# Chunk 1's keys crossed by GpSimd, a subtraction that restores the key order, and a new order of the first layers' calls, in a sorted-block attention with a two-layer MLP

## The chip, the cores and the metric

The kernel runs on one core of a Trainium2 chip. The metric is the device time of one execution in microseconds (us), lower is better. The engines are called PE (matmul), DVE (VectorE), ACT (ScalarE), POOL (GpSimd) and SP (SyncE, which here only issues DMAs).

## The reference

There are 4 batches, 8 heads, 768 positions and a head size of 64. Positions are cut into 8 blocks of 96. A small 8x8 matrix per head is balanced five times and mixes the blocks of keys and of values; each block of queries then attends to its mixed block. The result, as 3072 tokens of 512 numbers, goes through two matrix products with `h * cos(h)` between them.

```
P = sort_net
for _ in range(5):
    P = P - max(P, -1); P = exp(P)
    P = P / (sum(P, -1) + 1e-9); P = P / (sum(P, -2) + 1e-9)
k_sorted = einsum('bhij,bhjcd->bhicd', P, k_b)      # v_sorted likewise
scores = q_b @ k_sorted_b.T / sqrt(64)
attn = softmax(scores); x = attn @ v_sorted_b       # (3072, 512)
h = x @ w_in                                        # 512 -> 2048
out = (h * cos(h)) @ w_out                          # 2048 -> 512
```

## The kernel before

The tokens are worked in eight chunks of 384: chunk n is half of batch n // 2, four blocks of 96 tokens, called u. The order of all instructions is written out by hand; the engines run their own queues in that order and wait for each other by semaphores. PSUM is split into three "big" buffers of two banks (`B`) and two "acc" buffers of one bank (`C`), each handed out in turn.

For each chunk and block: `qk` (or two `qk_half`) makes scores on PE, DVE takes the maximum over the keys (`mx`, line 486) and subtracts it (`s`, line 487), `expo` writes exp of it to a `p_buf` on ACT (line 511), the result is turned (`p_transpose` on PE with a copy to `pT` by DVE or ACT in chunks 0 and 1, a DMA transpose issued by SP later), `av` multiplies it with the mixed values and DVE normalizes it (`r`, line 555, and `xn`, line 557), and `x_transpose` turns it into `xT`. Then `up(n, fp, lo, hi)` is an eighth of the first layer: PE makes `h` in a big buffer, ACT writes `c` = cos(h) (line 592), DVE multiplies `gg` = c * h (line 595). `down(n, ts, half)` is half of a 128-token tile of the second layer in an acc buffer, and ACT or DVE copies it out. In each chunk the attention of the next one is put between these calls. Chunk 0's first layer runs in two halves of columns (two blocks each), so that it can start before all its blocks are attended to.

Mixed keys: `k_products` makes for each pair of key positions t a [128, ...] block in PSUM whose partitions hold two neighbouring positions x of 64 head dimensions, for even and odd heads e. The tile `kTs` keeps them in three slots. A product for an even head reads slots 0 and 1, for an odd head slots 1 and 2, so slot 1 holds the other position of either kind, in the opposite partition half. For batch 0, `k_sort_0` copies from PSUM in four pieces of 64 partitions: chunk 0's with ih = 0, chunk 1's with ih = 1. `z_keys` zeroes on POOL the halves that these pieces leave out. For the later batches, `k_sort_1` and `k_sort_g` copy whole PSUM blocks into slots 0 and 2 and `k_swap` fills slot 1 by two DMAs.

Chunks 0 and 1 have the keys of a block in the order (x t), position parity first, in scores and in `s`; `expo` puts them back in the order (t x) as it writes.

Queries: `load_q(n)` loads a chunk by POOL-issued DMAs (one for chunks 0 to 2, eight from chunk 3 on). `q_transpose` turns chunks 0 to 2 on PE; `q_transpose_dma` on SP turns the later ones, after `zeros_between` on POOL. `load_pair` loads keys or values of batches 2 and 3, `v_permute` on POOL reorders values, and `hold_keys` is a tiny POOL copy that makes POOL wait for `k_swap`.

Of the kernel before, what the change touches and what calls it, by code (L numbers as in the profile page):

```python
# [18 lines left out]
def kernel(  # L19
# [75 lines left out]
    def load_pair(buf, src, lo, hi):  # L95

        nc.gpsimd.dma_start(
            out=buf[:, lo:hi], in_=src[2:4].rearrange("b r x -> (b r) x")[:, lo:hi])
# [187 lines left out]
    def copy_on(eng, dst, src):  # L286
        if eng is nc.scalar:
            eng.copy(dst, src)  # L288
        else:
            eng.tensor_copy(dst, src)  # L290
# [68 lines left out]
    def k_products(ps, t, c, rows, rhs, keys=kbuf):  # L359
        nc.tensor.matmul(  # L360
            ps[:, t], keys[rows, c * 2 * D:(c + 1) * 2 * D], rhs, start=True, stop=True)

    def k_sort_0(ih, t0, nt, eng, pool, tag):

        ps = pool.tile([128, nt, 2 * MH], FP32, name="ks", tag=tag)
        for t in range(nt):
            k_products(ps, t, t0 + t, slice(64, 128),
                       bds[0][64:, H:, ih * IC:(ih + 1) * IC])
        ms, ts = slice(ih * MH, (ih + 1) * MH), slice(t0, t0 + nt)
        psv = ps.rearrange("p t (e m) -> p e m t", e=2)  # L370
        for hp in range(2):
            for x in range(2):
                copy_on(eng, kT[0][hp * D:(hp + 1) * D, hp + x, ms, ts],
                        psv[x * D:(x + 1) * D, hp])

    k_open = {}

    def k_first(t0, nt, pool, tag):
        ps = pool.tile([128, nt, 2 * MH], FP32, name="ks", tag=tag)
        for t in range(nt):  # L380
            k_products(ps, t, t0 + t, slice(64, 128), bds[0][64:, H:, :IC])
        k_open[t0] = ps.rearrange("p t (e m) -> p e m t", e=2), slice(t0, t0 + nt)

    def k_place(t0, hp, eng):
        psv, ts = k_open[t0]
        for x in range(2):
            copy_on(eng, kT[0][hp * D:(hp + 1) * D, hp + x, :MH, ts],
                    psv[x * D:(x + 1) * D, hp])

    def k_sort_1(t0, eng, pool, tag):  # L390
        ps = pool.tile([128, 8, 2 * NB], FP32, name="ks", tag=tag)
        for t in range(8):
            k_products(ps, t, t0 + t, slice(0, 128),
                       bds[0][:, :H].rearrange("p x i -> p (x i)"))
        copy_on(eng, kT[1][:, ::2, :, t0:t0 + 8], ps.rearrange("p t (e m) -> p e m t", e=2))
# [26 lines left out]
    def scores(out, n, u, h2, hp):  # L422
        x = (u * H2 + h2) * blk
        if n == 0:
            rows = slice(hp * D, (hp + 1) * D)
            nc.tensor.matmul(
                out[:blk], q_of(0, 0)[rows, x:x + blk], keys_of(n, u, h2, hp)[rows],
                start=True, stop=True)
        else:

            nc.tensor.matmul(  # L431
                out, q_of(n, hp)[:, x:x + 128], keys_of(n, u, h2, hp), start=True, stop=True)
# [45 lines left out]
    def qk_part(n, u, part, pool, tag):  # L478
        w = len(part)
        sc = pool.tile([128, w, 512], FP32, name="sc", tag=tag)  # L480
        for h2 in range(H2):
            for e, hp in enumerate(part):
                scores(sc[:, e, h2 * blk:(h2 + 1) * blk], n, u, h2, hp)
        scv = sc[:blk, :, :H2 * blk].rearrange("p e (h c) -> p e h c", c=blk)
        mx = small.tile([blk, w, H2], FP32, name="mx", tag="mx")
        nc.vector.reduce_max(mx[:], scv, axis=AX.X)  # L486
        nc.vector.tensor_tensor(  # L487
            s_t[n, u][:, part[0]:part[0] + w], scv, mx.to_broadcast([blk, w, H2, blk]),
            op=ALU.subtract)

    def qk(n, u):

        s_t[n, u] = sp.tile([blk, 2, H2, blk], FP32, name="s", tag="s")
        qk_part(n, u, [0, 1], big, "big")

    def qk_half(n, u, hp, pool=acc, tag="acc"):

        if hp == 0:
            s_t[n, u] = sp.tile([blk, 2, H2, blk], FP32, name="s", tag="s")
        qk_part(n, u, [hp], pool, tag)  # L500

    def expo(n, u, on_pe=False):
        p = p_bufs[cnt[0] % NP]
        cnt[0] += 1


        dst, src = p[:, :, :blk], s_t.pop((n, u)).rearrange("p e h c -> p (e h) c")
        if n < 2:
            dst = dst.rearrange("p a (t x) -> p a x t", x=2)
            src = src.rearrange("p a (x t) -> p a x t", x=2)  # L510
        nc.scalar.activation(dst, src, AF.Exp, scale=scale)  # L511
        if n < LATE:
            t = ptp.tile([128, 2 * H2, blk], BF16, name="pT", tag="pT")
        else:

            z, w = (n * IC + u) % 8, 2 * H2 * blk
            t = vperm[:, z * w:(z + 1) * w].rearrange("p (a c) -> p a c", c=blk)
        pT[n, u] = t
        if on_pe:
            pb[n, u] = p  # L520
        else:
            nc.sync.dma_start_transpose(out=t[:], in_=p.rearrange("p a c -> p (a c)"))
# [8 lines left out]
    def p_transpose(n, u, eng, pool, tag):  # L531
        p = pb.pop((n, u))
        ps = pool.tile([128, 2 * H2, 128], BF16, name="pps", tag=tag)
        for a in range(2 * H2):
            nc.tensor.transpose(ps[:blk, a, :blk], p[:, a, :blk], ident[:blk, :blk])  # L535
        copy_on(eng, pT[n, u][:blk], ps[:blk, :, :blk])
# [44 lines left out]
    def up(n, fp, lo=0, hi=TC):  # L581

        h = big.tile([128, 2, 512], FP32, name="h", tag="big")
        w = hi - lo
        for f2 in range(2):
            f = fp * 2 + f2
            for kk in range(KC):
                nc.tensor.matmul(  # L588
                    h[:, f2, :w], w_in_t[:, kk, f * 128:(f + 1) * 128], xT[n][:, kk, lo:hi],
                    start=(kk == 0), stop=(kk == KC - 1))  # L590
        c = cosp.tile([128, 2, TC], FP32, name="c", tag="c")
        nc.scalar.activation(c[:, :, :w], h[:, :, :w], AF.Sin, bias=half_pi[:, 0:1])  # L592
        if lo == 0:
            gt[n, fp] = gp.tile([128, 2, TC], BF16, name="gg", tag="gg")
        nc.vector.tensor_tensor(  # L595
            gt[n, fp][:, :, lo:hi], c[:, :, :w], h[:, :, :w], op=ALU.mult)
# [62 lines left out]
        balance(1)  # L659
        spread(1)  # L660

    def z_keys():
        nc.gpsimd.memset(kT[0][64:, 0], 0.0)
        nc.gpsimd.memset(kT[0][:64, 2], 0.0)

    def z_vperm():
        nc.gpsimd.memset(vperm[:64, :D // 2 * blk], 0.0)

# [16 lines left out]
    load_w_out(1)  # L685
    load_w_out(2)
    load_w_out(3)
    k_sort_0(0, 0, 16, V, *C)
    v_turn()
    k_sort_0(0, 32, 8, V, *B)  # L690
    k_sort_0(0, 16, 16, A, *C)
    k_sort_0(0, 40, 8, A, *C)
    v_sort_b(0, 0, 8, A, *C)
    qk(0, 0)
    qk(0, 1)
# [22 lines left out]
    z_turned(0)  # L718
    last_balance()
    z_vperm()  # L720
    z_keys()
    p_transpose(0, 3, V, *C)
    up(0, 0, 0, 2 * blk)
    p_transpose(0, 2, V, *C)
    up(0, 1, 0, 2 * blk)
    av(0, 2, True)
    up(0, 2, 0, 2 * blk)
    k_sort_0(1, 0, 16, A, *C)
    av(0, 3, True)
    up(0, 3, 0, 2 * blk)  # L730
    x_transpose(0, 2, A, *C)
    up(0, 4, 0, 2 * blk)
    up(0, 5, 0, 2 * blk)
    x_transpose(0, 3, A, *C)
    k_sort_0(1, 16, 16, V, *C)
    up(0, 6, 0, 2 * blk)
    q_transpose(1, 0, (V, V), *C)
    up(0, 7, 0, 2 * blk)
    k_sort_0(1, 32, 16, A, *C)
    up(0, 0, 2 * blk, TC)  # L740
    q_transpose(1, 1, (V, V), *C)
    up(0, 1, 2 * blk, TC)
# [3 lines left out]
    up(0, 4, 2 * blk, TC)  # L746
    qk_half(1, 0, 1, *C)
    up(0, 5, 2 * blk, TC)
    qk_half(1, 1, 0, *C)
    load_q(2)  # L750
    up(0, 6, 2 * blk, TC)
    qk_half(1, 1, 1, *C)
    up(0, 7, 2 * blk, TC)
    load_pair(pair, kin_d, 0 * CD // 2, 1 * CD // 2)
    load_pair(pair, kin_d, 1 * CD // 2, 2 * CD // 2)
    v_permute(slice(64, 128))
    expo(1, 0, True)
# [6 lines left out]
    k_sort_1(8, A, *B)  # L764
    p_transpose(1, 1, A, *B)
    qk(1, 3)
    expo(1, 2, True)
    k_sort_1(16, A, *B)
    down(0, 1, 0, nc.sync)
    k_sort_1(24, A, *B)  # L770
    expo(1, 3, True)
    p_transpose(1, 2, A, *B)
    down(0, 1, 1, nc.sync, mid=[(av, 1, 1, True)])
    k_sort_1(32, V, *B)
    k_sort_1(40, A, *B)
    x_transpose(1, 0, V, *B)
    av(1, 2, True)
    p_transpose(1, 3, A, *B)
    k_swap(kT[1])
    down(0, 2, 0, nc.sync)  # L780
    x_transpose(1, 1, V, *B)
    av(1, 3, True)
    x_transpose(1, 2, V, *B)
    down(0, 2, 1, nc.sync, mid=[(x_transpose, 1, 3, V, *B)])
    q_transpose(2, 0, (V, V), *B)
    q_transpose(2, 1, (V, V), *B)
    zeros_between(3)
    hold_keys()
    load_pair(vbuf, vin_d, 0 * CD // 6, 1 * CD // 6)
    load_pair(vbuf, vin_d, 1 * CD // 6, 2 * CD // 6)  # L790
# [1 line left out]
    load_pair(vbuf, vin_d, 3 * CD // 6, 4 * CD // 6)  # L792
    load_pair(vbuf, vin_d, 4 * CD // 6, 5 * CD // 6)
    load_pair(vbuf, vin_d, 5 * CD // 6, 6 * CD // 6)
    load_q(3)
    up(1, 0)
    v_sort_b(1, 0, 8, A, *C)
    v_sort_b(1, 8, 8, A, *C)
# [28 lines left out]
    down(1, 1, 0, nc.sync)  # L827
    k_sort_g(8, A, *B)
    av(2, 0, True)
    expo(2, 3)  # L830
    p_hold(2, 3)
    down(1, 1, 1, nc.sync)
# [4 lines left out]
    x_transpose(2, 1, V, *B)  # L837
    av(2, 3, True)
    x_transpose(2, 0, V, *B)
    k_sort_g(16, A, *B)  # L840
    down(1, 2, 1, nc.sync, mid=[(k_sort_g, 20, A, *B), (x_transpose, 2, 2, V, *B), (x_transpose, 2, 3, V, *B)])
    load_q(4)
    q_transpose_dma(4)
# [107 lines left out]
```

## Time and profile before

| | |
|---|---|
| three runs | 245.69, 246.08, 246.58 us; median 246.08 |
| profiled execution | 245.58 us, span 243.8 us |
| mean granted clock of PE | 0.949 |
| busy in the span | PE 231.0, DVE 174.6, ACT 159.3, POOL 88.5 us |

Groups of instructions that the change touches (mean of one):

| group | count | ns |
|---|---|---|
| ACT `p_buf<-s` 96x768, all chunks | 32 | 896 |
| DVE `s<-sc,mx` 96x768 / 96x384 | 21 / 22 | 954 / 554 |
| DVE `mx<-sc` 96x768 / 96x384 | 21 / 22 | 947 / 547 |
| ACT `kTs<-ks` 64x256 | 12 | 367 |
| DVE `kTs<-ks` 64x256 | 8 | 421 |
| ACT / DVE `kTs<-ks` 128x512 | 16 / 2 | 581 / 684 |
| ACT / DVE `pT<-pps` 96x768 | 6 / 2 | 788 / 550 |
| POOL memset `kTs` 64x1536 | 2 | 1372 |
| POOL `vperm<-kv` 64x1536 | 6 | 2832 |
| POOL issue of `load_q` from chunk 3 on | 40 | 677 |

The profile is of one execution on the chip. Busy times are of one engine; PE's matmuls overlap, so a PE that is shown busy need not be at its best rate. The table by stage gives for each stretch of the span the busy time of each engine with the number of instructions, then the clock that PE was granted (1.00 is full), the busy share of the DMA engines and GB/s. The chain of waits follows the last instruction back to what released each step, so that only what stood on it made the execution longer. In the timeline, "idle before <- releaser" is how long the engine had waited and for whom. Several operations in one row are merged.

### The profile page before, as it was taken

How to read it: one execution, taken by the hardware profiler on the slowest of the kernel's cores; microseconds unless marked ns; L12 is line 12 of the kernel's file. 1: busy time of each engine (PE TensorE's matmuls, PEld its weight loads, DVE VectorE, ACT ScalarE, POOL GpSimd, SP SyncE). 2: the span in 40 equal slices, each digit the busy share in tenths (PEclk: the TensorE clock that was granted, in tenths of full speed). 3: DMA queues.
4: the chain of work that ended last, by engine and by line, in shares of the span. 5: the costliest groups of instructions: out<-in, count | busy, mean ns of one | idle time of the engine just before them, and what ended most of it. 6: DMA issues, size and time to landing. Idle time of an engine off the chain costs nothing.

```text
span 243.8 us, 5367 instructions
## 1 busy us (share of the span) xinstructions
PE 231.0 (95%) x2160; PEld 148.2 (61%) x2160; DVE 174.6 (72%) x323; ACT 159.3 (65%) x230; POOL 88.5 (36%) x106
## 2 busy tenths in 40 slices
PE   7979898789999989999999999999999999999994
PEld 5768787656566546665666656654565556446553
DVE  5569678994578956888568996898689768635700
ACT  4469877579288964889568866685568366726611
POOL 6359993399275999010354400800000000000000
PEclk9655599999999999999999999999999999999999
DMA  4999999991499878745798869945591480133012
GB/s 49 229 195 173 184 203 232 197 204 51 113 173 186 135 178 92 151 104 156 151 103 141 56 145 117 214 34 113 118 231 30 90 196 0 44 78 124 0 46 86
DMA packets 67897, 31.20 MB, mean 128 GB/s; under 512 B 56608, under 2 KB 63392, under 8 KB 67616
## 3 DMA queue, kind: packets, MB, share of 16 engines
q0 software_dynamic: 24048, 13.64, 41.1%
q1 hardware_dynamic: 43312, 17.02, 29.0%
q8 instruction: 17, 0.28, 0.5%
q10 hardware_dynamic: 512, 0.20, 0.3%
q14 instruction: 8, 0.07, 0.1%
HBM read 27.27 MB, written 6.29 MB: 138 GB/s over the span
## 4 chain that ended last, share of the span: by engine, by line
PE 78%; ACT 7%; DVE 7%; DMA 5%; issue 1%; SPq 0%; DVEq 0%; ACTq 0%
PE h L588 31%; PE o L612 28%; PE sc L431 4%; PE av L548 3%; PE ks L360 2%; ACT kTs L288 2%; PE pps L535 2%; DVE gg L595 2%; PE vs L464 2%; PE xps L575 1%; PE vs L454 1%; ACT p_buf L511 1%; ACT c L592 1%; DVE xn L557 1%; DMA pT<-p_buf 1%
## 5 line engine op out<-in xcount | busy, mean ns | idle before, releaser
L588 PE MATMUL h<-xT,w_in_t 128*128 128x384 bf16 (+1 forms) x576 | 92.3, 311 | 0.7 <-DMA xT<-xn 0.3
L612 PE MATMUL o<-w_out_t,gg 128*128 128x512 bf16 x368 | 88.0, 379 | 0.5 <-DVE s L487 0.5
L592 ACT ACTIVATE c<-h,half_pi 128x768 f32<-128x768 f32 (+1 forms) x72 | 59.7, 830 | 28.3 <-PE h L588 25.3
L595 DVE TENSOR_TENSOR gg<-c,h 128x768 bf16<-128x768 f32 (+1 forms) x72 | 61.2, 860 | 22.6 <-ACT c L592 22.5
L588 PEld LDWEIGHTS <-w_in_t 128*128 128x128 bf16 x576 | 53.3, 99 | 27.7 <-issue 1.5
L612 PEld LDWEIGHTS <-gg 128*128 128x128 bf16 x368 | 33.3, 98 | 32.4 <-DVE s L487 0.7
L487 DVE TENSOR_TENSOR s<-sc,mx 96x384 f32<-96x384 f32 (+1 forms) x43 | 32.2, 749 | 2.7 <-DVE mx L486 0.5
L486 DVE TENSOR_REDUCE mx<-sc 96x4 f32<-96x384 f32 (+1 forms) x43 | 31.9, 742 | 2.7 <-PE sc L431 1.4
L177 POOL COPY vperm<-kv 64x1536 bf16<-64x1536 bf16 (+1 forms) x10 | 28.1, 2842 | 5.4 <-DMA kv<-in_v_dram 5.4
L511 ACT ACTIVATE p_buf<-s 96x768 bf16<-96x768 f32 x32 | 27.7, 896 | 0.6 <-DVE s L487 0.2
L557 DVE TENSOR_TENSOR xn<-av,r 96x512 bf16<-96x512 f32 x32 | 22.0, 687 | 1.1
L288 ACT CAST kTs<-ks 128x512 bf16<-128x512 f32 (+2 forms) x32 | 14.7, 460 | 5.8 <-PE ks L360 5.6
L134 POOL DMA_DIRECT2D kv<-in_q_dram x24 | 16.1, 678 | 5.0 <-DMA kv<-in_v_dram 4.3
L431 PE MATMUL sc<-kTs,q_turned 128*128 128x96 bf16 x224 | 16.1, 206 | 0.9 <-DVE s L487 0.7
L555 DVE RECIPROCAL r<-av 96x8 f32<-96x8 f32 x32 | 6.4, 199 | 14.5 <-PE av L548 14.4
L431 PEld LDWEIGHTS <-q_turned 128*128 128x128 bf16 x224 | 12.8, 98 | 5.0 <-DVE s L487 1.3
L288 ACT COPY o_s<-o 128x512 f32<-128x512 f32 (+2 forms) x11 | 5.9, 538 | 14.8 <-PE o L612 11.8
L288 ACT COPY kv<-o 128x512 f32<-128x512 f32 x8 | 4.7, 583 | 12.6 <-PE o L612 12.6
L134 POOL DMA_DIRECT2D q_mem<-in_q_dram x16 | 10.6, 677 | 0.6 <-issue 0.6
L592 ACT ACT_TABLE_LOAD x8 | 10.3, 1283 | 0.1
L288 ACT CAST pair<-vs 96x512 bf16<-96x512 f32 (+1 forms) x12 | 8.7, 727 | 2.0 <-PE vs L464 2.0
L548 PEld LDWEIGHTS <-pT 96*128 96x128 bf16 (+1 forms) x160 | 7.3, 104 | 4.0 <-DMA pT<-p_buf 0.8
(102 smaller groups left out, 219.5 us busy)
## 6 DMA issues: line engine op xcount, KB each, us to landing
out_dram<-kv SPq DMA_DIRECT2D x12, 256.0 KB, 3.2
out_dram<-o_s SPq DMA_DIRECT2D x11, 256.0 KB, 2.4
w_in_t<-in_moe_w_in_dram POOLq DMA_DIRECT2D x4, 512.0 KB, 11.2
w_out_t<-in_moe_w_out_dram POOLq DMA_DIRECT2D x4, 512.0 KB, 13.3
kv<-in_k_dram POOLq DMA_DIRECT2D x2, 768.0 KB, 13.5
kv<-in_v_dram POOLq DMA_DIRECT2D x2, 768.0 KB, 15.1
pair<-in_k_dram POOLq DMA_DIRECT2D x2, 768.0 KB, 12.1
kv<-in_v_dram POOLq DMA_DIRECT2D x6, 256.0 KB, 7.3
```

The source lines that it names most:

```text
L134: nc.gpsimd.dma_start(out=q_heads[:, i, :, e], in_=src[:, ih * IC + i, :, e])
L177: nc.gpsimd.tensor_copy(dst, src)
L288: eng.copy(dst, src)
L431: nc.tensor.matmul(out, q_of(n, hp)[:, x:x + 128], keys_of(n, u, h2, hp), start=True, stop=True)
L486: nc.vector.reduce_max(mx[:], scv, axis=AX.X)
L487: nc.vector.tensor_tensor(s_t[n, u][:, part[0]:part[0] + w], scv, mx.to_broadcast([blk, w, H2, blk]), op=ALU.subtract)
L511: nc.scalar.activation(dst, src, AF.Exp, scale=scale)
L557: nc.vector.tensor_tensor(xn.rearrange("p h e d -> p e h d"), avv[:, :, :, :D], r.to_broadcast([blk, 2, H2, D]), op=ALU.mult)
L588: nc.tensor.matmul(h[:, f2, :w], w_in_t[:, kk, f * 128:(f + 1) * 128], xT[n][:, kk, lo:hi], start=(kk == 0), stop=(kk == KC - 1))
L592: nc.scalar.activation(c[:, :, :w], h[:, :, :w], AF.Sin, bias=half_pi[:, 0:1])
L595: nc.vector.tensor_tensor(gt[n, fp][:, :, lo:hi], c[:, :, :w], h[:, :, :w], op=ALU.mult)
L612: nc.tensor.matmul(o[:], gt[n, f // 2][:, f % 2, ts * 128:(ts + 1) * 128], w_out_t[:, f, :], start=(f == 0), stop=(f == FC - 1))
```

## The change

- Chunk 1's keys: `k_cross` copies the whole PSUM block of its products into slots 0 and 2 in one 128x512 copy, and two POOL copies of 64x256 fill slot 1 from them, across partition halves. It takes the place of `k_sort_0` with ih = 1. `z_keys` is dropped.
- Scores lie in PSUM at 128 words per head instead of 96. For chunks 0 and 1 the subtraction reads them in the order (t x), so `s` is in natural order, and the exponential reads and writes it straight.
- Reordered calls in the first layers of chunks 0 and 1; `p_transpose(0, 2)` copies on ACT instead of DVE.
- `load_q(3)` is issued ahead of `hold_keys` and the six value loads; `load_q(2)`, a pair load and `k_sort_g(16)` are placed earlier. On POOL, `load_q(2)` and the pair loads keep their place among POOL's instructions.

```diff
-    def k_sort_0(ih, t0, nt, eng, pool, tag):
+    def k_sort_0(t0, nt, eng, pool, tag):
...
-    def k_first(t0, nt, pool, tag):
...
-    def k_place(t0, hp, eng):
...
+    def k_cross(t0, nt, eng, pool, tag):
+        ps = pool.tile([128, nt, 2 * MH], FP32, name="ks", tag=tag)
+        for t in range(nt):
+            k_products(ps, t, t0 + t, slice(64, 128), bds[0][64:, H:, IC:])
+        ms, ts = slice(MH, 2 * MH), slice(t0, t0 + nt)
+        copy_on(eng, kT[0][:, ::2, ms, ts], ps.rearrange("p t (e m) -> p e m t", e=2))
+        nc.gpsimd.tensor_copy(kT[0][:D, 1, ms, ts], kT[0][D:, 0, ms, ts])
+        nc.gpsimd.tensor_copy(kT[0][D:, 1, ms, ts], kT[0][:D, 2, ms, ts])
...
-                scores(sc[:, e, h2 * blk:(h2 + 1) * blk], n, u, h2, hp)
-        scv = sc[:blk, :, :H2 * blk].rearrange("p e (h c) -> p e h c", c=blk)
-        mx = small.tile([blk, w, H2], FP32, name="mx", tag="mx")
+                scores(sc[:, e, h2 * 128:h2 * 128 + blk], n, u, h2, hp)
+        scv = sc[:blk].rearrange("p e (h c) -> p (e h) c", c=128)[:, :, :blk]
+        mx = small.tile([blk, w * H2], FP32, name="mx", tag="mx")
         nc.vector.reduce_max(mx[:], scv, axis=AX.X)
-        nc.vector.tensor_tensor(
-            s_t[n, u][:, part[0]:part[0] + w], scv, mx.to_broadcast([blk, w, H2, blk]),
-            op=ALU.subtract)
+        s = s_t[n, u][:, part[0]:part[0] + w].rearrange("p e h c -> p (e h) c")
+        if n < 2:
+            s, scv = (t.rearrange(o, x=2) for t, o in (
+                (s, "p a (t x) -> p a t x"), (scv, "p a (x t) -> p a t x")))
+        nc.vector.tensor_tensor(s, scv, mx.to_broadcast(list(s.shape)), op=ALU.subtract)
...
-        dst, src = p[:, :, :blk], s_t.pop((n, u)).rearrange("p e h c -> p (e h) c")
-        if n < 2:
-            dst = dst.rearrange("p a (t x) -> p a x t", x=2)
-            src = src.rearrange("p a (x t) -> p a x t", x=2)
-        nc.scalar.activation(dst, src, AF.Exp, scale=scale)
+        nc.scalar.activation(
+            p[:, :, :blk], s_t.pop((n, u)).rearrange("p e h c -> p (e h) c"), AF.Exp,
+            scale=scale)
...
     z_vperm()
-    z_keys()
     p_transpose(0, 3, V, *C)
     up(0, 0, 0, 2 * blk)
-    p_transpose(0, 2, V, *C)
+    p_transpose(0, 2, A, *C)
     up(0, 1, 0, 2 * blk)
     av(0, 2, True)
     up(0, 2, 0, 2 * blk)
-    k_sort_0(1, 0, 16, A, *C)
+    k_cross(32, 16, V, *C)
+    k_cross(0, 16, A, *C)
     av(0, 3, True)
...
     x_transpose(0, 3, A, *C)
-    k_sort_0(1, 16, 16, V, *C)
+    k_cross(16, 16, V, *C)
     up(0, 6, 0, 2 * blk)
     q_transpose(1, 0, (V, V), *C)
     up(0, 7, 0, 2 * blk)
-    k_sort_0(1, 32, 16, A, *C)
     up(0, 0, 2 * blk, TC)
...
+    load_q(2)
     qk_half(1, 1, 0, *C)
-    load_q(2)
     up(0, 6, 2 * blk, TC)
     qk_half(1, 1, 1, *C)
+    load_pair(pair, kin_d, 0 * CD // 2, 1 * CD // 2)
     up(0, 7, 2 * blk, TC)
-    load_pair(pair, kin_d, 0 * CD // 2, 1 * CD // 2)
...
     qk(1, 3)
+    k_sort_1(16, A, *B)
     expo(1, 2, True)
-    k_sort_1(16, A, *B)
     down(0, 1, 0, nc.sync)
     k_sort_1(24, A, *B)
     expo(1, 3, True)
     p_transpose(1, 2, A, *B)
-    down(0, 1, 1, nc.sync, mid=[(av, 1, 1, True)])
     k_sort_1(32, V, *B)
+    av(1, 1, True)
+    down(0, 1, 1, nc.sync, mid=[(av, 1, 2, True)])
     k_sort_1(40, A, *B)
     x_transpose(1, 0, V, *B)
-    av(1, 2, True)
     p_transpose(1, 3, A, *B)
     k_swap(kT[1])
     down(0, 2, 0, nc.sync)
-    x_transpose(1, 1, V, *B)
     av(1, 3, True)
     x_transpose(1, 2, V, *B)
+    x_transpose(1, 1, V, *B)
     down(0, 2, 1, nc.sync, mid=[(x_transpose, 1, 3, V, *B)])
...
     zeros_between(3)
+    load_q(3)
     hold_keys()
     load_pair(vbuf, vin_d, 0 * CD // 6, 1 * CD // 6)
...
     load_pair(vbuf, vin_d, 5 * CD // 6, 6 * CD // 6)
-    load_q(3)
...
     av(2, 0, True)
+    k_sort_g(16, A, *B)
     expo(2, 3)
...
     x_transpose(2, 0, V, *B)
-    k_sort_g(16, A, *B)
```

More of the change, by code (lines that the diff above doesn't have):

```diff
@@ L367, in k_sort_0 @@
             k_products(ps, t, t0 + t, slice(64, 128),
-                       bds[0][64:, H:, ih * IC:(ih + 1) * IC])
-        ms, ts = slice(ih * MH, (ih + 1) * MH), slice(t0, t0 + nt)
+                       bds[0][64:, H:, :IC])
+        ms, ts = slice(0, MH), slice(t0, t0 + nt)
         psv = ps.rearrange("p t (e m) -> p e m t", e=2)
@@ L374, in k_sort_0 @@
                         psv[x * D:(x + 1) * D, hp])
-    k_open = {}
-    def k_first(t0, nt, pool, tag):
+    def k_cross(t0, nt, eng, pool, tag):
         ps = pool.tile([128, nt, 2 * MH], FP32, name="ks", tag=tag)
         for t in range(nt):
-            k_products(ps, t, t0 + t, slice(64, 128), bds[0][64:, H:, :IC])
-        k_open[t0] = ps.rearrange("p t (e m) -> p e m t", e=2), slice(t0, t0 + nt)
-    def k_place(t0, hp, eng):
[L385 to L388, printed above, removed]
+            k_products(ps, t, t0 + t, slice(64, 128), bds[0][64:, H:, IC:])
[3 more added lines that the diff above has]
+        nc.gpsimd.tensor_copy(kT[0][D:, 1, ms, ts], kT[0][:D, 2, ms, ts])
     def k_sort_1(t0, eng, pool, tag):
@@ L660, in last_balance @@
         spread(1)
-    def z_keys():
-        nc.gpsimd.memset(kT[0][64:, 0], 0.0)
-        nc.gpsimd.memset(kT[0][:64, 2], 0.0)
     def z_vperm():
@@ L687 @@
     load_w_out(3)
-    k_sort_0(0, 0, 16, V, *C)
+    k_sort_0(0, 16, V, *C)
     v_turn()
-    k_sort_0(0, 32, 8, V, *B)
-    k_sort_0(0, 16, 16, A, *C)
-    k_sort_0(0, 40, 8, A, *C)
+    k_sort_0(32, 8, V, *B)
+    k_sort_0(16, 16, A, *C)
+    k_sort_0(40, 8, A, *C)
     v_sort_b(0, 0, 8, A, *C)
```

## The prediction

> **What bounds the kernel now.** I read the page first. TensorE (PE) is busy 95% of the span, so what can be won is PE's idle time, the time at a low clock, and the stages in which PE only follows another engine.
>
> ```profile
> PE 231.0 (95%) x2160; PEld 148.2 (61%) x2160; DVE 174.6 (72%) x323; ACT 159.3 (65%) x230; POOL 88.5 (36%) x106
> DVE  5569678994578956888568996898689768635700
> ```
>
> Then the table by stage (time, then busy us of PE, PEld, DVE, ACT, POOL). The change touches the stages up to 96 us.
>
> ```profile
> 13.00:28.70 15.70, 12.96 (x195) 11.23 (x193) 12.80 (x25) 13.26 (x26) 13.91 (x15) 0.50 1.14 180
> 36.00:42.50 6.50, 5.88 (x110) 5.00 (x108) 5.50 (x13) 4.80 (x11) 2.26 (x3) 1.00 1.16 228
> 42.50:49.20 6.70, 5.01 (x60) 4.02 (x59) 6.53 (x14) 3.66 (x7) 2.93 (x4) 1.00 1.12 201
> 67.50:81.00 13.50, 13.50 (x148) 9.02 (x148) 11.28 (x17) 11.63 (x17) 9.24 (x14) 1.00 1.18 162
> ```
>
> From 13 to 28.7 us PE runs at clock 0.50, and ACT is the fullest engine that computes. From 42.5 to 49.2 us, the end of chunk 0's first layer, DVE is full (6.53 of 6.70) and PE is not. From 67.5 us PE is full. The chain of waits from 12 to 70 us (start, us, what) says the same: ACT's exponentials, then DVE's work back to back.
>
> ```profile
> 19.98 0.97 ACT p_buf L511
> 23.20 0.97 ACT p_buf L511
> ...
> 37.85 0.43 DVE kTs L290
> ...
> 42.98 0.56 DVE q_turned L290
> 43.58 1.02 DVE gg L595 x2
> 44.59 0.47 DVE mx L486
> 45.09 0.55 DVE s L487
> 45.65 0.93 DVE gg L595 x2
> ...
> 50.62 1.08 ACT p_buf L511
> ```
>
> The timeline has the durations (the rows with x4 are four copies of 64x256 between partition halves):
>
> ```profile
> 19.87 1.07 ACT L511 ACTIVATE p_buf<-s 96x768 bf16<-96x768 f32 x1
> 37.42 1.72 DVE L290 CAST kTs<-ks 64x256 bf16<-64x256 f32 x4
> 39.80 1.50 ACT L288 CAST kTs<-ks 64x256 bf16<-64x256 f32 x4 [0.30 <-PE ks L360]
> 60.75 0.69 DVE L290 CAST kTs<-ks 128x512 bf16<-128x512 f32 x1 [0.17 <-PE ks L360]
> 80.04 3.59 SPq L147 DMA_TRANSPOSE q_turned<-kv  x2
> 83.73 3.14 SPq L522 DMA_TRANSPOSE pT<-p_buf  x2
> 85.39 0.84 ACT L511 ACTIVATE p_buf<-s 96x768 bf16<-96x768 f32 x1
> 90.26 0.68 PE L548 MATMUL av<-vS,pT 96*128 96x65 bf16 x16 [0.67 <-DMA pT<-p_buf]
> ```
>
> **Exponentials of chunk 0.** In chunks 0 and 1 the exponential scatters its bf16 output and takes 1.07 us; later chunks write it straight, 0.84. The change makes all eight straight: 0.23 less each. In chunk 0 two stand on the chain before the first attention product (19.98 and 23.20), so `av(0,0)` starts at 24.64 instead of 25.11 and the first `up` at 28.29 instead of 28.77: 0.48 won. The bounds are 0 and 0.48. The clock is 0.50 until about 31.2 us; should it open at the same moment as before, half of the 0.48 goes again, so I keep 0.25 as an uncertainty.
>
> **The subtraction** now reads PSUM in steps of 48 words and writes in order. No row has this access. The nearest are copies that read PSUM in steps of 64 words: `kTs<-ks` 128x512 on DVE takes 684 ns on average, the unstrided `o_s<-o` 128x512 takes 692. So I take nothing. Upper end: ACT's price for the same order, 0.23 per 96x768. A gain is excluded, as the element count stays. [...]
>
> **Chunk 1's keys.** Removed: twelve 64x256 copies (two groups on ACT, 1.50 each, one on DVE, 1.72). Added: three 128x512 copies (ACT 0.58, DVE twice 0.69) and six copies of 64x256 on POOL. `p_transpose(0,2)`'s copy leaves DVE (0.55) for ACT (0.80). DVE saves 1.72 + 0.47 - 1.36 = 0.8 us, ACT 3.00 - 0.58 - 0.80 = 1.6. PE's matmuls are the same. I walked the stage in the new order with these durations and the two accumulation and three big PSUM buffers, from `up` at 28.29:
> - `pT(0,2)` on ACT 30.32 to 31.12, done before PE wants it at 31.31.
> - DVE: gg 0 and 1 until 32.5, `xn(0,2)` until 33.37, gg 2, the first whole copy until 34.5, `xn(0,3)` until 35.36 (35.12 before, so the early copy costs something here, and `up(0,5)` waits until 35.40), gg 3 to 5 until 37.4, the second copy until 38.03, gg 6 until 38.74 (39.74 before).
> - Then two query copies (1.13), gg 7 and 8 with no idle time (0.57 before, as c waited behind ACT's 1.50 of key copies), two more query copies, and the next gg at 41.87 where it was 43.58.
>
> From here to 51.1 DVE has no gap before and gets none now, so 1.71 is won at this point, 1.23 of it in this stage. If PE or ACT set the pace instead, only the 0.8 of DVE remains.
>
> **POOL's six copies.** `vperm<-kv` 64x1536 takes 2.83 us, a one-element copy 0.19; by elements a 64x256 costs 0.63. Ends: 0.19 and 2.83. They run behind the vperm memset (ends 34.68), in place of two key memsets (1.37 each); the last pair starts when DVE's second copy ends (38.03) and is done at 39.4. PE's first `qk_half(1,0,0)` wants it at 41.05. Queued behind them on POOL is `load_q(2)`, which waits for PE's second query transpose (39.7) anyway. So nothing, and covered up to 1.26 each.
>
> **Exponentials of chunk 1 and the output layer.** PE waits 0.30 at 51.74 for `exp(1,0)`; 0.23 of it goes, and that product starts at 49.80 (1.94 won). The reordered calls from there: the wait of 0.21 at 55.77 stays, since the PSUM order there is unchanged; the one of 0.38 at 61.49 (`av` behind a DVE key copy) goes; a new one of 0.27 comes where `av(1,2)` in the middle of `down(0,1,1)` needs ACT's `pT` copy (58.1); `down(0,2,0)` starts at 60.0 (62.28 before). `xps(1,1)` ahead of the last half takes another 0.1. The second layer then starts at 65.1 instead of 67.50: 2.4 won.
>
> **Chunk 3's queries.** POOL reaches `load_q(3)` at 60.6 (its key permutation still starts at 47.4 with a DMA), issues eight times 0.68 until 66.0, then the hold and the six value loads at 66.2 (65.63 before). Of these `v_permute` takes the output, wanted by PE near 112 us: nothing. The gain is at SP: `q_transpose_dma(3)` sat there from 80.04 to 83.63 because its data came late, and chunk 2's first `pT` was queued behind it. That transpose now runs near 70 us; without the move an earlier PE would have met it and lost up to 2 us. At the new pace `pT` starts at 81.27, and its third at 85.14 lands 2.62 later, 87.76. `k_sort_g(16)` (0.23), moved ahead of this wait, fills part of it: 0.67 becomes 0.39. That is 0.3 won. ACT's copy for it delays `exp(2,3)`, which SP does not reach before 86.7.
>
> `load_q(2)` and the pair loads keep their order on POOL, the score layout of 128 words per head keeps the element counts: nothing. From 96 us PE is full and all later work follows it.
>
> **Sum.** 0.48 + 1.23 + 0.23 + 0.46 + 0.3 = 2.7 us. The profiled execution took 245.58 (span 243.8 and 1.8 around it), which is 0.5 under the median of 246.08. So 242.9 for such an execution, 243.4 for the median.
>
> **Rivals.**
> - *Only part of it*: PE, ACT or a buffer sets the pace in the first layer, or the clock opens late. Then 0.8 instead of 1.23 and 0.23 instead of 0.48, and the output layer's new wait of 0.27 doubles: 244.4 to 245.3. For it: in 36 to 42.5 us DVE is busy only 5.50 of 6.50. 0.13.
> - *The subtraction pays for its steps.* DVE's eight operations from 17.70 to 25.27 have no gap, and `r` of `av(0,0)` is next: four dearer subtractions delay it fully, four halves more lie in the full stretch from 44.5 on. At 0.23 each: 0.9 + 0.46, 244.8. At 0.5 each the gain is gone: 246.4. The copy rows of 684 and 692 ns speak against it, that none of them has two inputs or runs of two speaks for it. 0.10 for the case without gain. [...]
> - *Slower: POOL's crossing copies become the bound.* They run one after the other from 34.75. DVE needs scores by 42.85, so from 1.26 us each they delay the stage by six times the excess (34.75 + 6 x 1.26 = 42.3, and half a us for the scores); at 1.7 each the gain is gone, at 2.0 it is 4.4 us, 247.8; at a vperm copy's 2.83 it is 9.4 us, 252.8. Against it: that row has 6 times the elements. For it: no row shows POOL moving data between partition halves. 0.08.
> - A wait that I do not see, or an order that gives it back later: 0.05, slower.
>
> **Chances.** A measurement of this kernel can tell about 0.3% (0.74 us) from no change. My forecast, 242.0 to 244.4: 0.64. With the partial case faster is 0.77; same 0.10; slower 0.08 + 0.05 = 0.13. The range from 242.0 to 245.8 holds the forecast, the partial case and the mild end of the stepping subtraction.
>
> **What would show it.** Right: exponentials of 0.84 us everywhere, subtractions still 0.95 (96x768) and 0.55, POOL copies near 0.6, the first `up` near 28.3, the first `o` matmul of chunk 0 near 47.5, the second layer's first `h` near 65, `q_turned<-kv` on SP near 70, PE's wait for `pT` near 88 under 0.5. Wrong: subtractions above 1.1, a PE wait on POOL near 41, or DVE with idle time from 42 to 49.

## The result

The changed kernel took 245.55 us (median of 22 runs, 244.19 to 247.71), the kernel before 246.63 (22 runs beside them, 245.28 to 249.20): ratio 0.9948, 95% interval 0.9924 to 0.9971, so 1.1 us faster and not 2.7. In a second comparison (first experiment) the ratio was 0.9916 (0.9888 to 0.9945). The profiled execution has a span of 243.8 us, as before; all of its times are 0.08 later from the start on (first key product at 12.97, before 12.89).

### The profile page after: what moved, and what is told of

The parts are those of the page before. It is cut to its first block, busy times and chain, and to the rows that moved or that the text cites. A ratio compares the mean times of both kernels' runs of the same rounds, so it can differ in the third digit from the quotient of the medians.

```text
span 243.8 us, 5363 instructions
## 1 busy us (share of the span) xinstructions
PE 230.7 (95%) x2160; PEld 148.4 (61%) x2160; DVE 173.6 (71%) x320; ACT 156.2 (64%) x224; POOL 88.0 (36%) x110
## 4 chain that ended last, share of the span: by engine, by line
PE 77%; DVE 7%; ACT 7%; DMA 6%; issue 1%; ACTq 0%; SPq 0%; DVEq 0%
PE h L585 32%; PE o L609 27%; PE sc L427 3%; PE av L545 3%; PE ks L360 2%; DVE gg L592 2%; PE vs L450 2%; DMA vperm<-p_buf 2%; DMA pT<-p_buf 2%; PE vs L460 2%; DVE xn L554 1%; PE pps L532 1%; PE xps L572 1%; ACT p_buf L506 1%; PE sk L262 1%
## 5 line engine op out<-in xcount | busy, mean ns | idle before, releaser
L506 ACT ACTIVATE p_buf<-s 96x768 bf16<-96x768 f32 x32 | 25.9, 839 | 0.6 <-DVE s L488 0.4
L288 ACT CAST kTs<-ks 128x512 bf16<-128x512 f32 (+2 forms) x25 | 12.4, 496 | 6.5 <-PE ks L360 6.4
```

What stands on the lines that cost most here:

```text
L506: nc.scalar.activation(p[:, :, :blk], s_t.pop((n, u)).rearrange("p e h c -> p (e h) c"), AF.Exp, scale=scale)
```

## The profile after

The page: PE is as busy as before, DVE, ACT and POOL have a little less to do. The last line is the DMA queue that the page calls instruction, with 17 packets and 0.28 MB; they turn out to matter.

```profile
PE 230.7 (95%) x2160; PEld 148.4 (61%) x2160; DVE 173.6 (71%) x320; ACT 156.2 (64%) x224; POOL 88.0 (36%) x110
...
DVE  5569678986579955895768987896789769635700
...
q8 instruction: 17, 0.28, 0.5%
```

The table by stage (time, then busy us of PE, PEld, DVE, ACT, POOL, then the granted clock). From 36 us PE no longer idles (6.50 of 6.50, before 5.88), and the stretch in which DVE is full (6.54 of 6.70) has come 1.3 us earlier.

```profile
13.00:28.70 15.70, 13.36 (x197) 11.67 (x197) 12.95 (x26) 12.84 (x26) 13.57 (x14) 0.50 1.12 177
36.00:42.50 6.50, 6.50 (x110) 5.81 (x108) 5.57 (x12) 3.87 (x8) 3.43 (x7) 1.00 1.18 228
41.20:47.90 6.70, 5.16 (x64) 4.22 (x61) 6.54 (x14) 3.85 (x7) 1.29 (x3) 1.00 1.12 205
```

The groups, different shapes apart (count, then busy us and mean ns of one): the subtraction costs what it did (954 and 554 ns before), every exponential 839 ns, a crossing copy on POOL 396.

```profile
L506 ACT ACTIVATE p_buf<-s 96x768 bf16<-96x768 f32 x32 | 25.9, 839 | 0.6 <-DVE s L488 0.4
L488 DVE TENSOR_TENSOR s<-sc,mx 96x768 f32<-96x768 f32 x21 | 20.0, 954 | 1.6
L488 DVE TENSOR_TENSOR s<-sc,mx 96x384 f32<-96x384 f32 x22 | 12.2, 553 | 0.8
L383 POOL COPY kTs<-kTs 64x256 bf16<-64x256 bf16 x3 | 1.2, 396 | 1.6 <-DVE kTs L290 1.5
```

The chain of waits (start, us, what). The first `up` is at 28.48 (28.77 before), the gg that was at 43.58 at 42.27. New are two long transposes, 4.00 and 4.36 us from issue to landing, on which PE waits:

```profile
28.48 1.36 PE h L585 x8
...
42.27 1.02 DVE gg L592 x2
...
87.52 4.00 DMA pT<-p_buf
...
161.71 4.36 DMA vperm<-p_buf
```

The timeline of SP and PE around them (the bracket is PE's wait). The query transposes of chunk 3 leave SP by 80.5, the first pT starts at 81.83 (83.73 before), PE's wait of 0.67 before av(2,2) is gone. But av(2,3) now waits 1.09, and in chunk 4's output layer a product for chunk 5 waits 1.40, where the kernel before had no wait (its two lines stand last, with the other line numbers).

```profile
69.25 11.26 SPq L147 DMA_TRANSPOSE q_turned<-kv  x2
81.83 2.55 SPq L519 DMA_TRANSPOSE pT<-p_buf  x2
85.11 3.63 SPq L519 DMA_TRANSPOSE pT<-p_buf  x2
87.87 0.68 PE L545 MATMUL av<-vS,pT 96*128 96x65 bf16 x16
91.58 0.43 PE L545 MATMUL av<-vS,pT 96*128 96x65 bf16 x8 [1.09 <-DMA pT<-p_buf]
161.71 3.69 SPq L519 DMA_TRANSPOSE vperm<-p_buf  x2
166.11 0.43 PE L545 MATMUL av<-pair,vperm 96*128 96x65 bf16 x8 [1.40 <-DMA vperm<-p_buf]
...
163.25 2.83 SPq L522 DMA_TRANSPOSE vperm<-p_buf  x2
166.09 0.42 PE L548 MATMUL av<-pair,vperm 96*128 96x65 bf16 x8
```

**Where the time is, by segments.** PE's timeline alternates between `h` (first layer of a chunk, `up`) and `o` (output layer, `down`). In all traces here some segments take the same time (second layer's h to its o 13.07; h of chunk 5 to o of chunk 6 34.07, once 34.24; third layer's h to o of chunk 4 64.45, but for ph48 and ph96), so a kernel is described by six numbers, in us: **a** first key product to first h, **b** first h to first o, **c** first o to the second layer's h, **d** o of chunk 1 to the third layer's h, **e** o of chunk 4 to h of chunk 5, **f** o of chunk 6 to h of chunk 7. The last column is the time from the first h until the clock of PE opens, by the trace's clock records (at that moment the matmuls of h go from 160 to 82 ns from one start to the next).

| kernel | a | b | c | d | e | f | span | clock |
|---|---|---|---|---|---|---|---|---|
| before | 15.81 | 20.50 | 18.23 | 15.35 | 12.83 | 12.21 | 243.8 | 2.64 |
| rep_before | 15.79 | 21.35 | 18.23 | 16.59 | 12.87 | 11.79 | 245.9 | 5.11 |
| before_m8 | 15.80 | 20.69 | 18.25 | 16.20 | 13.89 | 12.12 | 245.7 | 3.51 |
| exp_only | 15.35 | 20.91 | 17.93 | 16.10 | 12.91 | 12.06 | 244.0 | 4.07 |
| after | 15.44 | 19.49 | 17.76 | 15.60 | 14.16 | 12.40 | 243.8 | 2.93 |
| rep_after | 15.36 | 20.08 | 17.76 | 16.11 | 12.83 | 12.25 | 243.5 | 5.39 |
| no_exp | 15.83 | 19.64 | 18.26 | 15.62 | 13.97 | 12.30 | 244.4 | 3.42 |
| no_order | 15.36 | 19.77 | 17.93 | 16.03 | 13.97 | 12.28 | 244.2 | 4.34 |
| lq3_back | 15.36 | 20.02 | 17.76 | 17.85 | 12.89 | 12.11 | 244.7 | 4.83 |
| k16_late | 15.37 | 19.70 | 17.76 | 15.16 | 13.96 | 12.27 | 243.0 | 4.19 |
| after_p8 | 15.36 | 20.09 | 17.76 | 15.79 | 12.89 | 12.22 | 243.3 | 5.10 |
| ph48 | 15.41 | 19.17 | 17.76 | 15.90 | 12.89 | 11.96 | 243.5 | 2.27 |
| ph96 | 15.81 | 20.08 | 17.76 | 16.22 | 12.83 | 11.77 | 245.1 | 5.08 |
| exp_early_p8 | 15.36 | 19.77 | 17.76 | 14.34 | 12.86 | 12.40 | 241.4 | 4.33 |

a, c and e have only a few values; d, e and f hold PE's waits for DMA transposes, and b grows with the last column (0.30 us for each us, by a straight line through the 14 traces).

## The experiments

**A second trace of each kernel**, without an edit, to see whether the long landings are chance.

> The changed kernel once more, for a second trace. Theory A (the early gain is real, and what is lost behind 90 us is lost at DMA transposes whose landing differs from execution to execution): the second layer again starts near 65.7 (before 67.50) and down(1,0,0) near 78.9, but the two waits of the first trace (1.09 at 91.6 for pT, 1.40 at 166.1 for vperm) do not both come back; the landings of 4.0 and 4.4 us are found at other transposes or not at all, and the span is anywhere from 242.4 to 244.5. Theory B (the change itself makes these transposes late): both waits come back at the same places with 1 us or more each, and up(5,0) starts again at 173.1 or later. Time by both: 0.4 to 0.6% under the kernel before.

> The kernel before once more, for a second trace of it. Theory A: its transposes too have landings of 4 us and more at one place or another, so its waits from 87 to 220 us differ from those of the first trace (0.67 at 90.3, none at 166) by half a us or more in at least one place. Theory B: the same landings (2.6 us) and the same waits as in the first trace, up(5,0) at 173.3 within 0.3.

Measured: the changed kernel 245.34 us, ratio 0.9916 (0.9888 to 0.9945), more than the 0.4 to 0.6% that both theories expected; the kernel before 247.66, one run. The second layer of the changed kernel started at 66.42 and not near 65.7: the trace begins its key products 0.24 later, and b is 0.59 longer, as the clock opened later. The wait for the fourth pT came back (1.60, landing 4.5), the one for vperm did not.

```profile
85.86 3.64 SPq L519 DMA_TRANSPOSE pT<-p_buf  x2
...
92.85 0.43 PE L545 MATMUL av<-vS,pT 96*128 96x65 bf16 x8 [1.60 <-DMA pT<-p_buf]
162.98 3.04 SPq L519 DMA_TRANSPOSE vperm<-p_buf  x2
```

The second trace of the kernel before waits 0.99 and 0.75 in segment d where the first waited 0.67. So neither theory holds as it stood. The wait at 91 belongs to the change: the fourth pT of chunk 2 lands after 4.0 to 4.5 us in all six traces of the changed order whose PE program is not shifted (after, rep_after, no_exp, no_order, k16_late, lq3_back), and after 2.6 in all four of the old order (before, rep_before, exp_only, before_m8). The one at 166 comes and goes.

**The natural order alone, and all but it.**

In exp_only the kernel before gets the change's `scores` and subtraction and the straight exponential; no_exp undoes these lines in the changed kernel, but for the layout of 128 words:

```diff
+        if n < 2:
+            s, scv = (t.rearrange(o, x=2) for t, o in (
+                (s, "p a (t x) -> p a t x"), (scv, "p a (x t) -> p a t x")))
...
-        if n < 2:
-            dst = dst.rearrange("p a (t x) -> p a x t", x=2)
-            src = src.rearrange("p a (x t) -> p a x t", x=2)
```

> The kernel before with only the natural order by subtraction (scores of 128 words per head, straight exponentials in chunks 0 and 1). Theory A: exponentials 0.84 instead of 1.07, subtractions 954 and 554 ns as before, first up at 28.3 to 28.5 (28.77 before), the wait of 0.30 at 51.7 down to under 0.1, second layer at 66.8 to 67.0 (67.50): 0.5 to 0.7 us early there, and 0.1 to 0.3% of the time if half of it survives. Rival (the steps of 48 words cost something where the engines are full): subtractions above 1.0 us, no gain at the second layer.

> The changed kernel without the natural order by subtraction: the exponentials of chunks 0 and 1 scatter again (1.07 us each), all else as changed. Theory A: first up at 28.8, the first o matmul of chunk 0 at 48.2 to 48.4 (47.90 with it, 49.20 before), second layer at 66.2 to 66.5 (65.73 with it, 67.50 before): the keys and the reordered calls bring 1.0 to 1.3 us of the 1.77 there. Rival (the exponentials bring nearly all): second layer at 67.0 or later.

Measured: exp_only 246.48 us, ratio 0.9970 (0.9942 to 0.9998), first `up` at 28.16 and second layer at 66.99; no_exp 246.08, ratio 0.9962 (0.9937 to 0.9988), first o at 48.26 and second layer at 66.53. These lie in the first theory's intervals or within 0.03 of them, but for the first `up` of exp_only, which came 0.14 before its interval. The exponentials bring 0.45 in a and 0.30 in c, the keys and the order most of b. The subtractions of exp_only take 954 and 553 ns, so the rival of a dear subtraction is out.

**What makes a transpose land late.** Some transposes that land after 2.6 us in one trace take 4.0 to 4.6 in another. The DMA records of after show what the fourth pT (issued 87.52) meets: its 256-byte packets, 18 ns each, start at 88.7; just then one packet of 16384 bytes on the instruction queue starts and takes 1.36 us; some transpose packets then take 1.4 to 1.6 us each, and the last third moves only from 90.7 on. The trace has 17 such packets for the 4345 instructions of PE (2160 matmuls, 2160 weight loads and 25 others), one for about 256; no other engine has more than 363. The transpose that met this one took 4.00 us to land. The DMA queues and the issue of after from 88 to 89.5 us:

```profile
q8 instruction: 1, 0.02, 5.7%
...
pT<-p_buf SPq DMA_TRANSPOSE x1, 4.0
```

If that is the cause, shifting PE's program by some instructions must move the late landings. `keep_warm` makes the idle matmuls at the start; it gets their width as a second argument here. The edit for ph48; in ph96 it is (64, 64), and the numbers are matmuls and columns:

```diff
-    keep_warm(16)
+    keep_warm(40, 102)
```

> As ph96, with 40 idle matmuls of 102 columns: 48 more PE instructions. Theory P: the packet that fell at 88.7 comes near 87.2, into the third pT transpose of chunk 2 (issued at 85.1, landing 4 us instead of 2.6), so PE waits about 1.2 us for that one, at av(2,2) near 88, and not for the fourth; the packet of 163.7 comes near 160.7, ahead of the vperm transposes, so no wait there. Rival C: the wait for the fourth stays at 1.1 us or more, and none appears at the third.

> The changed kernel with the 16 idle matmuls of 256 columns at the start split into 64 of 64 columns: the same columns, 96 more PE instructions (48 matmuls and 48 weight loads) ahead of everything. The DMA records show one 16 KB instruction packet for each 256 PE instructions. Theory P (a transpose lands at 4.0 to 4.6 us instead of 2.6 when such a packet falls into its transfer): every packet comes 96 instructions earlier in the program, the one at 88.7 at about 84.8, the one at 163.7 at about 157.8, the one at 214.2 at about 208; the fourth pT transpose of chunk 2 lands after 2.6 us and PE waits under 0.2 for it (1.09 and 1.60 so far), no wait for vperm near 166, up(7,0) 0.2 to 0.4 nearer to the end of the layer before it; 1.2 to 2.5 us of the time, 0.985 to 0.990 of the kernel before. Rival C (the late landing comes from the transposes' own order: the fourth is issued after a pause of 1.16 us): the wait of 1.1 to 1.6 us stays and the time is that of the changed kernel.

Measured: ph48 245.25 us (one run); ph96 245.99, ratio 0.9930 (0.9901 to 0.9959). In ph48 the packet starts at 86.9, the third pT (issued 85.02) lands after 4.26 us, the fourth after 2.71, and the wait has moved from av(2,3) to av(2,2); vperm lands after 2.63 and nothing waits there:

```profile
85.02 3.63 SPq L519 DMA_TRANSPOSE pT<-p_buf  x2
...
89.32 0.68 PE L545 MATMUL av<-vS,pT 96*128 96x65 bf16 x16 [1.39 <-DMA pT<-p_buf]
91.79 0.42 PE L545 MATMUL av<-vS,pT 96*128 96x65 bf16 x8
163.13 2.55 SPq L519 DMA_TRANSPOSE vperm<-p_buf  x2
```

ph96 freed the fourth pT, the first vperm of chunk 5 and the xT ahead of the last layer as expected (2.58, 2.67 and 2.33), but gained nothing: chunk 3's second query transpose held SP until 82.98 (80.5 in after) and landed at 86.25, the packet came at 86.3 among the pT behind it, and av(2,0) waited 1.71; another packet at 145.9 cost 0.68. Its a is also 0.4 longer than in after (15.81 against 15.44), for a reason that stays open. In ph48 two pT of chunk 3 landed after 5.28 and 4.57, and the third layer's h to o took 1.2 longer. So the late landings moved with the packets, as Theory P says, and the expected gain was missed because the shift of all packets traded one collision for another.

Counted over all 14 traces the picture is the same. They have 490 transposes to pT, vperm and xT. In 66 of them an instruction packet starts between 0.95 and 2.3 us after the issue, and all 66 land after 3.7 to 4.7 us; of the other 424 only nine take 3.7 or more.

**Chunk 3's queries back behind the value loads.**

```diff
     zeros_between(3)
-    load_q(3)
...
     load_pair(vbuf, vin_d, 5 * CD // 6, 6 * CD // 6)
+    load_q(3)
```

> The changed kernel with load_q(3) back behind the six value loads. My step: the two query transposes of chunk 3 then sit on SP until their data have come (near 80), chunk 2's first pT is queued behind them and starts at 83.5 to 84 instead of 81.8, av(2,0) and av(2,2) wait together 1.5 to 2 us, and the third layer starts 1 to 2 us later than in the changed kernel. Rival: the value loads in front cost the query loads little, the transposes end before 81.8 and nothing is lost (under 0.3 us).

Measured: 246.68 us, ratio 0.9974 (0.9948 to 0.9999), segment d 17.85 against 15.60 and 16.11. The first pT starts at 84.45 behind the query transposes, a little later than expected. The first two waits are 1.91 and 0.47, together 2.38 where 1.5 to 2 were expected; a third of 0.61 is for the fourth pT, which met a packet here too:

```profile
80.72 3.63 SPq L147 DMA_TRANSPOSE q_turned<-kv  x2
84.45 3.12 SPq L519 DMA_TRANSPOSE pT<-p_buf  x2
87.80 0.43 PE L545 MATMUL av<-vS,pT 96*128 96x65 bf16 x8 [1.91 <-DMA pT<-p_buf]
```

The moved load is worth 1.7 to 2.3 us at the pace of the changed kernel; the prediction had said up to 2.

**The exponential ahead of the key copy.**

```diff
+    expo(2, 3)
     k_sort_g(16, A, *B)
-    expo(2, 3)
```

> The changed kernel with k_sort_g(16) called just behind expo(2, 3) instead of ahead of it, so that ACT makes the exponential before that copy. Theory P: exp(2,3) ends 0.5 us earlier, the fourth transpose is issued 0.8 to 1.1 earlier, right behind the third (86.5 where it was 87.5), and either escapes the packet at 88.7 (no wait) or is hit and lands by 90.7 (wait 0.2 to 0.6): 0.5 to 1.1 us won in this stage. Rival C: issued without a pause it lands after 2.6 us in any case, no wait, and no other transpose of the run has a landing of 4 us that an instruction packet explains.

Measured: 244.01 us, ratio 0.9873 (0.9834 to 0.9913). The fourth pT is issued at 86.98, 0.5 earlier and not the 0.8 to 1.1 expected, and, with the packet at 89.0, lands after 4.10: hit, as Theory P allows, with a wait of 0.65 (I had 0.2 to 0.6). A pause of 0.60 is left ahead of it, so this run alone does not speak against Rival C; ph48 does, where the pause is 1.14 and the landing 2.71. Segment d is 15.16, 0.44 to 0.95 better than in the two traces of the changed kernel.

**The race near 162 us.** Behind 96 us the two kernels' PE programs are the same, but the changed one has 22 semaphore instructions where the other has 25. The edit for after_p8; before_m8 has (12, 341) in the kernel before:

```diff
-    keep_warm(16)
+    keep_warm(20, 205)
```

> The changed kernel with 20 idle matmuls of 205 columns at the start in place of 16 of 256: 8 PE instructions more. Behind 96 us its PE program is that of the kernel before, with 3 instructions fewer ahead of it (22 semaphore instructions for 25), so each packet comes 3 PE instructions later in the work. Theory P: the packet near 162 is a race with the first vperm transpose of chunk 5, which both kernels meet within 0.1 us; in the kernel before it goes first (163.2 against the issue at 163.25), in the changed kernel it loses in two traces of three and falls into the transfer. With 8 instructions more it comes 0.4 us earlier, goes first, the transpose lands at 2.6 to 2.9, and the wait near 166 (1.40, 1.20, 1.19) is gone: o to h of chunk 4 takes 12.9 us instead of 14.0 to 14.2, and the median falls by 0.5 to 1. The wait for the fourth pT near 91 stays. Rival: the late landing there has another cause, the stage takes 14.0 in about half of the traces.

> The kernel before with 12 idle matmuls of 341 columns in place of 16 of 256: 8 PE instructions fewer. Theory P: its packet near 163 comes 0.4 us later, loses the race and falls into the first vperm transpose of chunk 5: landing 4.1 to 4.4 instead of 2.7, a PE wait of 1.0 to 1.4 near 168, o to h of chunk 4 14.0 instead of 12.8, and the median 0.3 to 1.2 us above the kernel before. Rival: no such wait, the time that of the kernel before.

Measured: after_p8 245.11 us, ratio 0.9922 (0.9890 to 0.9954), e 12.89, the packet at 162.6 and the first vperm issued at 162.68, landing 2.60, no wait. before_m8 247.49, ratio 1.0019 (0.9987 to 1.0051), e 13.89: vperm issued at 164.18, the packet only at 166.2, landing 4.08, and the wait stands in the kernel before, which had none:

```profile
164.18 3.49 SPq L522 DMA_TRANSPOSE vperm<-p_buf  x2
...
168.31 0.43 PE L548 MATMUL av<-pair,vperm 96*128 96x65 bf16 x8 [1.12 <-DMA vperm<-p_buf]
```

Both stages came as Theory P says, each in one trace, and the other traces fit. The first vperm transpose of chunk 5 is issued 2.94 us after the first o of chunk 4 in all 14. In seven (before, rep_before, exp_only, rep_after, lq3_back, after_p8, exp_early_p8) the packet starts 2.8 to 3.1 us after that o, and the landing takes 2.6 to 3.1. In five (after, no_exp, no_order, k16_late, before_m8) it starts at 4.8 to 4.9, and the landing takes 4.1 to 4.4. In ph48 and ph96 it has passed before the issue. None starts in between, so a packet that does not come first seems to be held up by the transposes, which was not tested. The medians did not come as it says: after_p8 is no faster than the changed kernel (0.9916 on another chip) and before_m8 not measurably slower than the kernel before, though its lowest run (246.93) is 1.3 above the lowest of that (245.67, 24 runs).

**The output layer's old order.**

```diff
+    expo(1, 2, True)
     k_sort_1(16, A, *B)
-    expo(1, 2, True)
...
+    down(0, 1, 1, nc.sync, mid=[(av, 1, 1, True)])
     k_sort_1(32, V, *B)
-    av(1, 1, True)
-    down(0, 1, 1, nc.sync, mid=[(av, 1, 2, True)])
...
+    av(1, 2, True)
...
+    x_transpose(1, 1, V, *B)
     av(1, 3, True)
     x_transpose(1, 2, V, *B)
-    x_transpose(1, 1, V, *B)
```

> The changed kernel with the output-layer calls of chunk 0 (k_sort_1(16), av(1,1), av(1,2), x_transpose(1,1)) back in the order of before. From the first o matmul of chunk 0 to the second layer's first h: 18.24 before, 17.76 changed. My step (the reordered calls bring 0.2 to 0.46 there): 18.0 to 18.2. Rival (they bring nothing, the exponentials bring it all): 17.7 to 17.8. In the median under 0.3 us either way.

Measured: 244.83 us, ratio 0.9908 (0.9870 to 0.9947); c 17.93. Between the two expectations: the order brings 0.17 (c 17.76 with it), the exponentials 0.30, together the 0.47 measured.

**A version that beats both**: the exponential as early as its scores, and the 8 instructions.

```diff
     down(1, 1, 0, nc.sync)
+    expo(2, 3)
     k_sort_g(8, A, *B)
...
-    expo(2, 3)
```

> after_p8 with expo(2, 3) called ahead of k_sort_g(8), where its scores are ready (85.47): the fourth pT transpose of chunk 2 is issued right behind the third, at 86.5 instead of 87.5. Theory P: it lands by 89.1, or by 90.5 if the packet near 88.5 hits its end, PE wants it at 90.5: wait 0 to 0.1 (1.09 in the changed kernel), third layer at 93.3 to 93.5; with the wait near 166 gone too the span is 241.5 to 242.5 and the time 0.980 to 0.986 of the kernel before, below every kernel so far. Rival: what is won here is given back at another transpose, 0.987 to 0.992.

Measured: 243.27 us (6 runs, 242.73 to 244.29), ratio 0.9848 (0.9811 to 0.9886), span 241.4, third layer at 93.11. The two transposes are issued back to back, the fourth lands after 2.60, and PE waits for neither. It was close: the packet started at 88.90, 0.2 us before that landing at 89.11, and came too late to hold it:

```profile
85.15 2.59 SPq L519 DMA_TRANSPOSE pT<-p_buf  x2
...
87.91 0.67 PE L545 MATMUL av<-vS,pT 96*128 96x65 bf16 x16
...
90.37 0.42 PE L545 MATMUL av<-vS,pT 96*128 96x65 bf16 x8
```

## Why the prediction was right in direction and 1.6 us too large

Right, with the numbers beside the steps:
- **Exponentials of chunk 0**, 0.48: a fell by 0.43 (mean of 15.44 and 15.36 against 15.80).
- **The subtraction**, nothing: 954 and 553 ns against 954 and 554. In chunks 0 and 1, where it reads PSUM in steps of 48 words, each takes 0.95 or 0.55 us in after, as in the later chunks; the rival's 0.23 and 0.5 us more for each show in no run.
- **POOL's copies** cost 396 ns, not 630; the last ends at 39.15 and PE never waits for them. `load_q(3)` ahead of the values is worth what was said (lq3_back), and the wait for the third pT is gone.

Short in the traces, each by a little:
- **The first layer**, 1.23: b fell by 1.0, from the mean of 20.50, 21.35 and 20.69 to that of after, rep_after, no_order, k16_late, after_p8, lq3_back and exp_early_p8 (19.85). But these traces differ in the moment at which the clock opens. Where it opens alike, b differs by 1.26 (rep_before and after_p8), 1.21 (exp_only and k16_late) and 1.05 (before_m8 and no_exp); a straight line through all 14 traces gives 1.19 for the change and 0.30 us of b for each us by which the clock opens later. So the size was right, and 0.2 was lost to the clock, which opened 4.44 us after the first h on average in the seven traces of the changed order and 3.75 in the three of the old. The prediction had kept 0.25 for this as an uncertainty. The walk was right in order, but in after xn(0,3) ended at 35.56 where I had 35.36, and DVE then idled 0.49 and 0.28 where I had it full.
- **The reordered calls of the output layer**, 0.46: 0.17. The wait behind DVE's key copy went and the new gap behind ACT's pT copy came as foreseen, but no_order shows that the sum of the two is worth less than half.
- **The walk to the third layer**: d fell from 15.35, 16.59, 16.20 (mean 16.05) to 15.60 and 16.11 (15.86), 0.2 instead of 0.3. I let the fourth pT follow from the third and said that SP does not reach `exp(2,3)` before 86.7. It ended at 87.50, the transpose went out at 87.52, and the packet met it there. With the exponential early d is 14.34, 1.5 less, in the one trace in which the packet just missed.

So at 96 us the gain is 0.43 + 1.0 + 0.47 + 0.2 = 2.1 us of the 2.7.

The step that failed is the sentence **"From 96 us PE is full and all later work follows it."** PE is full, but SP's transposes have a partner that I left out, the instruction packets. Their place moves with the count of PE instructions ahead (48 more in ph48 brought the one at 88.7 to 86.9), which the cost of the moved calls does not tell. The kernel before has the same 17 packets, and four of its pT, vperm and xT transposes land after 4.1 to 4.5 us, but PE waits for one of them only, 0.27; so its waits did not show them.

Between the first traces of the two kernels the segments add up: the changed one is 0.37 shorter in a, 1.01 in b and 0.47 in c, and 0.25 longer in d, 1.33 in e and 0.19 in f. With the start 0.08 later that is 1.85 won and 1.85 lost, and both spans are 243.8. The largest loss, e, is the wait of 1.40 for the late vperm.

Over several traces, e of the changed order at the unshifted count took 14.16, 13.97, 13.97 and 13.96 (after, no_exp, no_order, k16_late), and 12.83 and 12.89 (rep_after, lq3_back): mean 13.63, where before, rep_before and exp_only took 12.87. That is 0.76 lost. In f the mean of the same six is 12.27 against 12.02, another 0.25; but in f the xT transpose lands late in both kernels and the traces overlap, so that these 0.25 belong to the change is not shown. 2.1 - 0.76 - 0.25 = 1.1 us, which is the median's gain in the first comparison; that it fits so well is in part luck, as the means are of few traces and the second comparison showed 2.2. There the changed kernel took nearly the same (245.34 against 245.55), and the kernel before 247.54 instead of 246.63; in the two sessions after it, without the changed kernel, it took 247.30 and 247.60. So the two comparisons differ in the kernel before, and why was not settled; by the second one only 0.5 of the 2.7 is missing. What share of all runs loses the race near 162 was not settled either: four of six traces lost it, and the medians of after_p8 and before_m8 could not tell. That the three instructions are what tips it is likewise argued from the two shifts by 8, not shown by a shift of 3.

## What to carry to other kernels

Where PE is full and reads what a DMA transpose delivers, look at the landing of each transpose and not at the median: 2.6 and 4.1 us stand side by side here, and the instruction packets say which is which (all 66 transposes that met one were late, and 9 of the 424 others). The reordering moved these meetings even where it changed no work: behind 96 us the PE programs are the same, and e went from 12.83 to 14.16 between the first traces. What can be tried is slack between landing and use: the exponential issued two copies earlier left 1.26 us (89.11 to 90.37), and a late landing adds 1.1 to 2.1 here. That slack alone would do was not shown, as the packet missed in that trace. Judge such a change by segments of several traces, since one span (243.8 in both kernels here) may hide 2 us won and 2 us lost.

## What the runs showed of the hardware that I had not expected

A packet of 16384 bytes on the instruction queue takes 0.88 to 1.88 us in before and 0.92 to 1.64 in after, which have 17 of them each. The 66 transposes of the 14 traces in which such a packet started 0.95 to 2.3 us after the issue landed after 3.7 to 4.7 us; the median landing in after is 2.6 us for pT and vperm and 2.4 for xT.

The granted clock of a table can be wrong by a factor of two. In rep_after the table by stage gives 1.00 for 13 to 28.7 us, in after 0.50, and in both the first eight h take 1.44 us; the eight that take 0.83 with full clock come first at 31.71 in after and at 34.79 in rep_after. The trace of rep_after has no clock record before 33.95 us, and the table counts a stretch without a record as full clock. So the clock is checked against the matmuls' durations. The moment of opening lies between 30.9 and 34.2 us in the 14 traces. The table by stage of rep_after:

```profile
13.00:28.70 15.70, 13.11 (x196) 11.44 (x196) 12.94 (x27) 12.94 (x26) 14.05 (x15) 1.00 1.16 181
```

The timeline of PE of the same execution:

```profile
28.57 1.44 PE L585 MATMUL h<-xT,w_in_t 128*128 128x192 bf16 x8
30.45 1.48 PE L585 MATMUL h<-xT,w_in_t 128*128 128x192 bf16 x8
32.21 1.47 PE L585 MATMUL h<-xT,w_in_t 128*128 128x192 bf16 x8
34.79 0.83 PE L585 MATMUL h<-xT,w_in_t 128*128 128x192 bf16 x8
```

The same rows of after:

```profile
28.40 1.44 PE L585 MATMUL h<-xT,w_in_t 128*128 128x192 bf16 x8
30.29 1.33 PE L585 MATMUL h<-xT,w_in_t 128*128 128x192 bf16 x8
31.71 0.83 PE L585 MATMUL h<-xT,w_in_t 128*128 128x192 bf16 x8
```
